# Two products of a gate/value round change places, and one subtraction moves ahead of a multiplication

## The chip, the core and the metric

The kernel runs on one core of a Trainium2 chip. The core has five engines, each with an instruction stream of its own: TensorE (PE; its weight loads are shown apart as PEld), VectorE (DVE), ScalarE (ACT), GpSimd (POOL) and SyncE (SP), whose queue issues most of the DMAs. They wait for one another through semaphores. What counts is the time of one execution on the device, in microseconds (us).

## What is computed

A DeltaNet recurrence (4 sequences, 8 heads, 768 tokens, head size 48) feeds a SwiGLU block (3072 tokens, 384 wide, 1536 inner). All values are fp32.

```python
def _attn_ref(q, k, v, beta):
    k_n = k / (np.linalg.norm(k, axis=-1, keepdims=True) + 1e-06)
    state = np.zeros((B, H, D, D), dtype=np.float32)
    for t in range(S):
        kt, vt, bt = (k_n[:, :, t], v[:, :, t], beta[:, :, t, None])
        y[:, :, t] = np.einsum('bhd,bhde->bhe', q[:, :, t], state)
        v_old = np.einsum('bhde,bhd->bhe', state, kt)
        state = state + bt[:, :, :, None] * np.einsum('bhd,bhe->bhde', kt, vt - v_old)
    return y

def _moe_ref(x, w_gate, w_val, w_out):   # x: y, heads side by side
    g = x @ w_gate
    silu = g * (1.0 / (1.0 + np.exp(-g)))
    return silu * (x @ w_val) @ w_out
```

## The kernel before

The 768 tokens are worked in 12 chunks of 64 (C), all four sequences at a time, so a chunk is 256 tokens. While the feed-forward part of chunk c runs, the attention of chunk c + 1 and the preparation of later chunks are woven into it: `point` and `point_and_fill` (lines 1757 to 1770) are places in the program at which one step of attention is issued, where one is due. The order of all instructions on all engines is written out by hand (`manual_schedule`, line 1807), so it is the order of the calls in the code.

The first two chunks use plain products with the gate and value weights while the weights are still being loaded and converted. From chunk 2 on (FAST) the gate and value products are made with a bilinear scheme that needs fewer products: for a round r, three blocks of 256 gate and value columns (`PAIRS[r]`), two halves of the chunk's tokens and three parts of the 384 rows are combined through sums of weights, sums of x and sums of partial results. There are two rounds in each of chunks 3 to 11 and one in chunk 2: 19 in all (`gate_val_fast`, line 1328).

A round consists of products numbered 0 to 14. `multiply(p, n, c, r)` (line 1291) issues product n: `product4` (line 1278) makes four fp32 matmuls of 128x128 weights by 128 tokens onto the four quarters of the PSUM bank p; in the trace each is two loads and two matmuls, so a product is eight of each, all on line 1280. Unless told to start afresh, a product adds onto what the bank holds. Products 1, 6, 7, 8, 9 and 12 (FORMS) read sums of weights that are reloaded from DRAM through a ring of four buffers; using one issues the DMA of a later one on SP's queue (line 1209). The other products, 0 and 5 among them, read blocks of `w_gv`, which stays in SBUF.

A round works in four PSUM banks: p4 (later called p2), p3 (later p6), p0 and p1 (later p5). `t0` and `t1` are 128x512 buffers in SBUF (`p_sb` in the trace; in the first round `last_h` and `h_f`). VectorE's `plus` and `minus` (lines 1506 to 1510) combine banks and buffers; their instructions are all on lines 1510 and 1507. `finish_h(c, r, e, p)` (line 1312) turns a finished bank into a piece of the hidden layer: ScalarE takes silu of the gate half (line 1316), VectorE multiplies it with the value half (line 1317).

The part of a round that matters here (lines 1357 to 1373), in words: products 7 (onto p1), 11 (onto p0) and 9 (onto p2); VectorE makes t1 = t1 - p0 behind product 11; product 0 completes bank p3 and product 5 adds onto p0; silu and multiplication finish p3; VectorE makes p5 = t0 - p0, which needs product 5, and p6 = t0 - p2, which overwrites bank p3. Then comes a point at which attention may be issued, and products 6 (onto p0), 10 (onto p5) and 8 (onto p6). These three wait for VectorE: 6 and 10 for the subtraction into p5, 8 for the one into p6. Product 5 overwrites what t1 = t1 - p0 reads, and waits for that. `load_late` (line 1349 and further on) issues a load of v on SP's queue when one is waiting there. Attention products read and write two pairs of banks of their own, `p_px` and `p_py`.

Behind the rounds, `output_fast` (line 1541) multiplies the hidden layer with the output weights in seven products (line 1557).

Of the kernel before, what the change touches and what calls it, by code (L numbers as in the profile page):

```python
# [20 lines left out]
def kernel(  # L21
# [327 lines left out]
    def load_late():  # L349
        if late_loads:  # L350
            late_loads.pop(0)()
# [811 lines left out]
    def new_h(c, f, at):  # L1163
        hs[c, f] = hp[at].rearrange("p (i n) -> p i n", i=2)
# [5 lines left out]
    def units(t):  # L1170
        return t.rearrange("p (u n) -> p u n", u=4)
# [17 lines left out]
    def block(k, r, n):  # L1189
        f = PAIRS[r][n]  # L1190
        return w_gv[:, :, k, 128 * f : 128 * f + 256]
# [8 lines left out]
    def form(n, c, r):  # L1200
        if c == FAST:
            return made_in[r][n]
        return slot(turns.index((c, r, n)))
# [7 lines left out]
    def used(n, c, r):  # L1211
        if c > FAST:
            reload(turns.index((c, r, n)) + len(ring))
# [35 lines left out]
    def x_of(c, tok_, k):  # L1249
        return xts[c][:, k, 128 * tok_ : 128 * tok_ + 128]  # L1250

    def x_less(c):
        return hp[4][:, 0:128] if c == FAST else x_of(c, 0, 0)
# [24 lines left out]
    def product4(p, w, moving, start=False):  # L1278
        for u in range(4):
            nc.tensor.matmul(  # L1280
                p[:, u], w(u), moving, start=start and u == 0, stop=True,
                skip_group_check=True,
            )
# [7 lines left out]
    def multiply(p, n, c, r, start=False):  # L1291

        if n in FORMS:
            t = units(form(n, c, r))
            w = lambda u: t[:, u]
        else:
            x = block(BLOCK[n][0], r, BLOCK[n][1])
            w = lambda u: x[:, u // 2, 128 * (u % 2) : 128 * (u % 2) + 128]
        if n == 11:
            moving = x_less(c)  # L1300
        else:
            moving = x_of(c, *PLAIN_X[n]) if n in PLAIN_X else sums_x[n]
        product4(p, w, moving, start)
        if n in FORMS:
            used(n, c, r)

    def temps(c, r):
        if (c, r) == (FAST, 0):
            return units(hp[13]), units(hp[5])
        return units(p_places[0][:, 0:HW]), units(p_places[0][:, HW : 2 * HW])  # L1310

    def finish_h(c, r, e, p):

        n = parts["sil"] = 1 - parts["sil"]
        silu_of = sil[:, n].rearrange("p (i n) -> p i n", i=2)
        nc.scalar.activation(silu_of, p[:, 0:2], ACTF.Silu)  # L1316
        nc.vector.tensor_tensor(  # L1317
            out=h_of(c, PAIRS[r][e % 3], e // 3), in0=silu_of, in1=p[:, 2:4], op=ALU.mult
        )
# [8 lines left out]
    def gate_val_fast(c, r, fill):  # L1328

        parts["x used"] = True  # L1330
        p4, p3, p0, p1 = (units(ffn_banks[i]) for i in parts["g"])
        p2, p6, p5 = p4, p3, p1
        t0, t1 = temps(c, r)
        assert (c, r) == (FAST, 0) or steps("join", 1) >= 4
        for f in PAIRS[r]:
            new_h(c, f, f // 2)

        tail = parts["tail"]
        if tail is not None:
            multiply(p4, 4, c, r, True)  # L1340
            nc.scalar.copy(p0, p4)
            tail[0]()
            multiply(p3, 13, c, r, True)
            nc.scalar.copy(t0, p3)
        multiply(p0, 1, c, r)
        if tail is not None:
            tail[1]()
        multiply(p4, 3, c, r)
        load_late()
        multiply(p3, 2, c, r)  # L1350
        nc.scalar.copy(t1, p4)
        plus(p1, p0, t0)
        plus(p2, p3, t1)
        if r > 0:
            sums_of_h(c, 6)
        point_and_fill(c + 1, 2.5, fill)
        multiply(p1, 7, c, r)
        multiply(p0, 11, c, r)
        nc.scalar.copy(t0, p1)
        multiply(p2, 9, c, r)  # L1360
        minus(t1, t1, p0)
        multiply(p3, 0, c, r)
        load_late()
        multiply(p0, 5, c, r)
        finish_h(c, r, 5, p3)
        minus(p5, t0, p0)
        minus(p6, t0, p2)
        point_and_fill(c + 1, 2.5, fill)
        multiply(p0, 6, c, r)
        multiply(p5, 10, c, r)  # L1370
        plus(t1, t1, p0)
        load_late()
        multiply(p6, 8, c, r)
        finish_h(c, r, 4, p5)
        finish_h(c, r, 1, p0)
        multiply(p2, 14, c, r)
        if r > 0:
            sums_of_h(c, 10)
        finish_h(c, r, 0, p6)
        finish_h(c, r, 3, p2)  # L1380
        if r > 0:
            sums_of_h(c, 8)
        point_and_fill(c + 1, 2.5, fill)

        def last():
            multiply(p6, 12, c, r)
            plus(t1, p6, t1)

        parts["tail"] = last, lambda: finish_h(c, r, 2, t1)
        a, b, m, d = parts["g"]  # L1390
        parts["g"] = (d, a, m, b)
# [114 lines left out]
    def minus(out, a, b):  # L1506
        nc.vector.tensor_tensor(out=out, in0=a, in1=b, op=ALU.subtract)  # L1507

    def plus(out, a, b):
        nc.vector.tensor_tensor(out=out, in0=a, in1=b, op=ALU.add)  # L1510
# [21 lines left out]
    def sums_of_h(c, f):  # L1532
        f1 = f - FH
        plus(s_of(f1), h_of(c, f1, 1), h_of(c, f, 1))
        minus(h_of(c, f1, 1), h_of(c, f1, 0), h_of(c, f1, 1))
# [147 lines left out]
    def steps(kind, *args):  # L1683
        return gens.get((kind, args), (None, 0))[1]
# [72 lines left out]
    def point_and_fill(c, n, fill):  # L1757
        spent.clear()
        point(c)
        fill(n - sum(spent))  # L1760
# [46 lines left out]
    with tc.manual_schedule(  # L1807
# [133 lines left out]
        for c in range(2, NCH):  # L1941
            if c > FAST:
                begin(c)
            point(c + 1)
            if c == FAST:
                begin(c)
            gate_val_fast(c, 0, fill)
            if c > FAST:
                gate_val_fast(c, 1, fill)
            else:  # L1950
                gate_val_plain(c, fill)
            output_fast(c, fill)
            finish(c + 1)
            x_sums(c + 1)
# [30 lines left out]
```

## Time and profile before

| what | value |
|---|---|
| median of 3 runs | 687.78 us (686.82 to 689.39) |
| the profiled execution | 689.76 us |
| its span, first to last instruction | 688.1 us |
| mean granted TensorE clock | 0.992 |
| matmuls of line 1280 by `x_t` with `w_gv` | 760, 102.4 us busy, 278 ns each |
| VectorE, middle and last subtraction of a round (`ffn<-p_sb,ffn`) | 36, 692 ns each |
| silu on ScalarE, line 1316 (`sil<-ffn`) | 95, 382 ns each |
| multiplication behind it, line 1317 (`h_f<-sil,ffn`) | 95, 418 ns each |

The profile is that of one execution. "Busy" is time in which an engine has work; matmuls are pipelined and overlap, so a busy TensorE is not one at its peak. The start of a weight load tells best when TensorE comes to a product. In the views, a line of a group or of the timeline gives engine, line of the code, operation, output and inputs by their names in the program, shape and count; what stands in square brackets is how long the engine was idle before, and what ended that.

### The profile page before, as it was taken

To read this page: it belongs to the slowest core of one execution; us is meant where nothing else is said; L and a number is where in the kernel's file an instruction comes from. 1 tells how busy PE (TensorE), PEld (TensorE's weight loads), DVE (VectorE), ACT (ScalarE), POOL (GpSimd) and SP (SyncE) were. 2 spreads that over 40 slices of the span, in tenths; PEclk is the share of its full clock that TensorE was granted. 3 is DMA by queue.
4 is the path that set the end of the run, shared out by engine and by line. 5 is a ranking of instruction groups with operands and counts; after the bars stand their busy time and mean duration, and the time that the engine had idled before them with its cause. 6 is when DMAs were issued, how large, how long until landed. Compare 5 with 4: busy or idle time off the path is not lost.

```text
span 688.1 us, 24813 instructions
## 1 busy us (share of the span) xinstructions
PE 653.7 (95%) x10850; PEld 603.7 (88%) x10850; DVE 473.3 (69%) x982; ACT 256.1 (37%) x546; POOL 201.7 (29%) x309
## 2 busy tenths in 40 slices
PE   7788999998999999999999999999999999999997
PEld 4566888756988899999999999999999999999997
DVE  7987778798569867757767747767657655645462
ACT  5785765214332332334332244332232333132130
POOL 7130031104883030881030881030882000000000
PEclk9998999999999999999999999999999999999999
DMA  9767824016226352276262176242187122132220
GB/s 135 169 176 190 243 94 137 1 35 136 45 45 164 73 136 64 49 156 143 54 134 74 45 153 138 60 110 80 26 171 152 48 88 78 40 100 71 76 71 23
DMA packets 147437, 68.55 MB, mean 100 GB/s; under 512 B 123457, under 2 KB 126561, under 8 KB 147329
## 3 DMA queue, kind: packets, MB, share of 16 engines
q1 hardware_dynamic: 144992, 66.48, 40.2%
q8 instruction: 85, 1.39, 0.8%
q10 hardware_dynamic: 2080, 0.39, 0.4%
q0 software_dynamic: 256, 0.10, 0.1%
q14 instruction: 24, 0.19, 0.1%
HBM read 59.08 MB, written 7.86 MB: 97 GB/s over the span
## 4 chain that ended last, share of the span: by engine, by line
PE 64%; DVE 3%; issue 0%; DVEq 0%
PE ffn L1280 36%; PE ffn L1557 17%; PE p_px L1073 1%; PE p_px L1054 1%; PE p_py L497 1%; PE p_py L1127 1%; PE p_py L1044 1%; DVE x_t L1510 1%; DVE ffn L1507 1%; PE p_px L902 1%; PE p_px L497 1%; PE p_py L1152 1%; PE p_py L884 1%; PE p_px L870 1%; DVE o_sb L1510 0%
## 5 line engine op out<-in xcount | busy, mean ns | idle before, releaser
L1280 PE MATMUL ffn<-x_t,w_gv 128*128 128x128 f32 x760 | 102.4, 278 | 6.6 <-DVE x_t L1507 6.6
L1280 PEld LDWEIGHTS ffn<-x_t,w_gv 128*128 128x128 f32 x760 | 93.1, 193 | 8.3 <-issue 5.8
L1557 PE MATMUL ffn<-wo_sb,h_f 128*128 128x192 f32 x480 | 84.2, 329 | 0.6 <-ACT ffn L1549 0.6
L811 POOL TENSOR_TENSOR n_b<-mb,half 128x32 f32<-128x32 f32 x5 | 27.6, 5520 | 191.3 <-DVE mb L551 191.3
L1280 PE MATMUL ffn<-x_ffn,w_gv 128*128 128x128 f32 x600 | 80.0, 277 | 0.0
L1557 PEld LDWEIGHTS ffn<-wo_sb,h_f 128*128 128x128 f32 x480 | 77.8, 190 | 1.6 <-ACT ffn L1549 0.9
L1316 ACT ACTIVATE sil<-ffn 128x256 f32<-128x256 f32 x95 | 34.5, 382 | 114.6 <-PE ffn L1280 106.6
L586 POOL TENSOR_TENSOR zb<-zb,h_f 128x31 f32<-128x31 f32 (+15 forms) x124 | 71.9, 580 | 9.7
L1280 PEld LDWEIGHTS ffn<-x_ffn,w_gv 128*128 128x128 f32 x600 | 73.8, 194 | 0.0
L580 POOL TENSOR_TENSOR h_f<-zb,mb 128x31 f32<-128x31 f32 (+15 forms) x124 | 69.4, 560 | 14.4 <-DVE mb L568 5.0
L1280 PE MATMUL ffn<-x_t,h_f 128*128 128x128 f32 x464 | 63.6, 280 | 3.9 <-DVE ffn L1507 3.9
L1317 DVE TENSOR_TENSOR h_f<-sil,ffn 128x256 f32<-128x256 f32 x95 | 37.6, 418 | 42.8 <-ACT sil L1316 42.8
L1280 PEld LDWEIGHTS ffn<-x_t,h_f 128*128 128x128 f32 x464 | 56.3, 192 | 5.9 <-DVE ffn L1507 4.9
L1440 PE MATMUL ffn<-x_ffn,w_gv 128*128 128x256 f32 x216 | 48.0, 381 | 0.0
L1440 PEld LDWEIGHTS ffn<-x_ffn,w_gv 128*128 128x128 f32 x216 | 40.7, 190 | 5.6
L1510 DVE TENSOR_TENSOR o_sb<-o_sb,ffn 128x192 f32<-128x192 f32 x49 | 17.1, 349 | 31.5 <-PE ffn L1557 31.0
L1510 DVE TENSOR_TENSOR ffn<-ffn,p_sb 128x512 f32<-128x512 f32 x36 | 24.8, 693 | 16.2 <-PE ffn L1280 15.1
L1557 PE MATMUL ffn<-last_k,h_f 128*128 128x192 f32 x200 | 35.8, 326 | 0.0
L1440 PE MATMUL ffn<-x_t,w_gv 128*128 128x256 f32 x144 | 35.7, 400 | 0.0
L1557 PEld LDWEIGHTS ffn<-last_k,h_f 128*128 128x128 f32 x200 | 32.8, 190 | 0.0
L1440 PEld LDWEIGHTS ffn<-x_t,w_gv 128*128 128x128 f32 x144 | 27.7, 199 | 4.0
L1280 PE MATMUL ffn<-x_ffn,h_f 128*128 128x128 f32 x224 | 30.0, 277 | 0.0
(343 smaller groups left out, 1165.2 us busy)
## 6 DMA issues: line engine op xcount, KB each, us to landing
h_f<-w_s SPq DMA_DIRECT2D x81, 256.0 KB, 2.7
more_w<-w_s SPq DMA_DIRECT2D x27, 256.0 KB, 2.9
vin<-in_v_dram SPq DMA_DIRECT2D x48, 96.0 KB, 3.5
out_dram<-o_sb SPq DMA_DIRECT2D x48, 96.0 KB, 2.2
kn<-in_k_dram SPq DMA_DIRECT2D x20, 192.0 KB, 4.7
w_s<-h_f SPq DMA_DIRECT2D x10, 256.0 KB, 3.2
zt<-in_moe_w_out_dram SPq DMA_DIRECT2D x6, 384.0 KB, 4.4
qpad<-in_q_dram SPq DMA_DIRECT2D x36, 64.0 KB, 3.2
```

The costliest lines, as they stand in the source:

```text
L497: nc.tensor.matmul(p_v[par][half_of(b if of_q else b ^ par), bp, j], kt[c][half_of(par), bp, j, b], xt[half_of(par), bp, j, b],)
L580: engine.tensor_tensor(out=t_v, in0=zb[:, 0 : j + 1, j : j + 1].to_broadcast([128, j + 1, m]), in1=mb[:, j : j + 1, j + 1 : R].to_broadcas ...
L586: engine.tensor_tensor(out=zb[:, 0 : j + 1, j + 1 : R], in0=zb[:, 0 : j + 1, j + 1 : R], in1=t_v, op=ALU.add,)
L811: nc.gpsimd.tensor_tensor(out=n, in0=mb.rearrange("p j i -> p (j i)")[:, 0 : R * R : R + 1], in1=half, op=ALU.pow,)
L870: nc.tensor.matmul(p_j[dst, c, m], a[lo, c, 2 * m + e, 0:R], zt[lo, c, 2 * m + e, R:C],)
L884: nc.tensor.matmul(p_j[hi, e, c, m], z1[row, c, m], t2[row, c, m])
L1280: nc.tensor.matmul(p[:, u], w(u), moving, start=start and u == 0, stop=True, skip_group_check=True,)
L1316: nc.scalar.activation(silu_of, p[:, 0:2], ACTF.Silu)
L1317: nc.vector.tensor_tensor(out=h_of(c, PAIRS[r][e % 3], e // 3), in0=silu_of, in1=p[:, 2:4], op=ALU.mult)
L1440: nc.tensor.matmul(ps[name][:, i], w_sb[:, t, (f + i) * 128 : (f + i + 1) * 128], xts[c][:, t], start=(t == 0 and i == 0), stop=(t == KT - 1),
L1510: nc.vector.tensor_tensor(out=out, in0=a, in1=b, op=ALU.add)
L1557: nc.tensor.matmul(p[x, part], a(f - f % 2)[:, f % 2], b(f), start=not begun and f == 0, stop=f == FH - 1, skip_group_check=True,)
```

## The change

In every round products 0 and 5 change places, and with them the order of the VectorE instructions behind them: p5 = t0 - p0 stands ahead of the multiplication of `finish_h(c, r, 5, p3)` instead of behind it. The late load stands between the two products as before.

```diff
         nc.scalar.copy(t0, p1)
         multiply(p2, 9, c, r)
         minus(t1, t1, p0)
+        multiply(p0, 5, c, r)
+        load_late()
         multiply(p3, 0, c, r)
-        load_late()
-        multiply(p0, 5, c, r)
+        minus(p5, t0, p0)
         finish_h(c, r, 5, p3)
-        minus(p5, t0, p0)
         minus(p6, t0, p2)
         point_and_fill(c + 1, 2.5, fill)
         multiply(p0, 6, c, r)
```

The instructions of ScalarE, GpSimd and SyncE keep their order; TensorE's and VectorE's change in the 19 rounds only, and their number stays.

## The prediction

> **What bounds the kernel now.** I read the page first: busy times, then the chain that ended last.
>
> ```profile
> PE 653.7 (95%) x10850; PEld 603.7 (88%) x10850; DVE 473.3 (69%) x982; ACT 256.1 (37%) x546; POOL 201.7 (29%) x309
> PE 64%; DVE 3%; issue 0%; DVEq 0%
> ```
>
> TensorE (PE) sets the time; VectorE (DVE) enters the chain only here and there. So the question is where TensorE stands still. The view of its waits, largest first:
>
> ```profile
> PE ffn L1280 <- DVE ffn L1507: 7.9, 10, 0.8
> PE ffn L1280 <- DVE x_t L1507: 6.6, 5, 1.8
> ```
>
> Ten times a product of line 1280 waits for a subtraction of line 1507. The timeline of one such round, in order of time (start, length, engine); I count from product 9's first weight load, 618.27:
>
> ```profile
> 618.27 0.97 PEld L1280 LDWEIGHTS ffn<-x_t,h_f 128*128 128x128 f32 x8
> 618.58 0.69 DVE L1507 TENSOR_TENSOR p_sb<-p_sb,ffn 128x512 f32<-128x512 f32 x1 [0.23 <-PE ffn L1280]
> 619.17 0.97 PEld L1280 LDWEIGHTS ffn<-x_ffn,w_gv 128*128 128x128 f32 x8
> 620.06 0.97 PEld L1280 LDWEIGHTS ffn<-x_t,w_gv 128*128 128x128 f32 x8
> 620.37 0.38 ACT L1316 ACTIVATE sil<-ffn 128x256 f32<-128x256 f32 x1 [2.10 <-PE ffn L1280]
> 620.78 0.42 DVE L1317 TENSOR_TENSOR h_f<-sil,ffn 128x256 f32<-128x256 f32 x1 [1.51 <-ACT sil L1316]
> 621.26 1.29 DVE L1507 TENSOR_TENSOR ffn<-p_sb,ffn 128x512 f32<-128x512 f32 x2
> 622.01 0.97 PEld L1280 LDWEIGHTS ffn<-x_t,more_w 128*128 128x128 f32 x8 [0.98 <-DVE ffn L1507]
> 622.01 1.16 PE L1280 MATMUL ffn<-x_t,more_w 128*128 128x128 f32 x8 [0.79 <-DVE ffn L1507]
> 622.90 0.97 PEld L1280 LDWEIGHTS ffn<-x_t,w_gv 128*128 128x128 f32 x8
> ```
>
> The loads are products 9, 0, 5, 6, 10. A product holds TensorE 0.89 (619.17 to 620.06). Product 6 would load at 620.95 and loads at 622.01: a pause of **1.06**. Why: VectorE starts on a product's result 1.20 after that product's first load (620.06 to 621.26; 622.01 to 623.21 for the next one agrees), the middle subtraction (p5 = t0 - p0) takes 0.69, and TensorE's load follows 0.06 after its end (621.95 to 622.01). Product 5 is directly in front of product 6, so 1.20 + 0.69 + 0.06 = 1.95 must pass where 0.89 is covered. The multiplication ends at 621.20, just as product 5's result is ready, so today it costs nothing.
>
> There are 19 rounds (18 + 1 first subtractions in the answer on line 1507):
>
> ```profile
> L1507 DVE TENSOR_TENSOR p_sb<-p_sb,ffn x18: 686/687/690, 239.6 to 661.8; 128x512 f32<-128x512 f32 x18
> L1507 DVE TENSOR_TENSOR h_f<-h_f,ffn x1: 689/689/689, 182.5 to 182.5; 128x512 f32<-128x512 f32 x1
> ```
>
> I went through all in the timeline. **Ten are open** (product 9 at 182.2, 239.3, 312.2, 343.3, 416.3, 447.3, 519.3, 618.3, 647.1, 661.5): nothing stands between products 5 and 6, and each shows the picture above. **Nine are filled**: TensorE has 1.1 to 2.2 us of attention products there and shows no pause. In six of these, and in all open ones, the first subtraction (t1 = t1 - p0) runs from 0.31 to 1.00. In three (256.5, 360.6, 464.6) it is late:
>
> ```profile
> 255.90 1.22 DVE L888 COPY zt<-p_py 32x1024 f32<-32x1024 f32 x1 [0.70 <-ACT zt L888]
> 256.54 0.97 PEld L1280 LDWEIGHTS ffn<-x_t,h_f 128*128 128x128 f32 x8
> 257.16 0.69 DVE L1507 TENSOR_TENSOR p_sb<-p_sb,ffn 128x512 f32<-128x512 f32 x1
> ```
>
> A copy of 1.22 stands in front, and the subtraction ends at 257.85, 1.31 after product 9's load.
>
> **The change, step by step.** No instruction is added or removed, and no DMA: products 5 and 0 take weights that stay in w_gv, so they issue no reload, and the late load keeps its place in SP's queue between the reloads of products 9 and 6. ScalarE's order is the same. What moves is the wait of product 5 (it adds onto p0, so it waits for the first subtraction): it loses its cover, product 0. Behind it in TensorE's queue is everything.
>
> *Open round.* The first subtraction ends at 1.00, so product 5 loads at 1.06 instead of 0.89: new pause 0.17. Product 0 loads at 1.95. The middle subtraction starts at 1.06 + 1.20 = 2.26, with no multiplication ahead of it, and ends at 2.95; product 6 loads at 3.01. By TensorE's own pace it would be 1.95 + 0.89 = 2.84, so a second pause of 0.17. Before, product 6 loaded at 622.01 - 618.27 = 3.74. Gain **0.73**, ten times: 7.3.
>
> Next late would be product 8, which overwrites p3 and waits for the last subtraction. Silu starts at 1.95 + 1.20 = 3.15, the multiplication 0.41 later (620.37 to 620.78), ends at 3.98; the subtraction starts 0.03 after it (617.92 behind a 0.42 operation at 617.47, where one VectorE operation waits for another), ends at 4.70, product 8 could load at 4.76. TensorE comes to it at 3.01 + 2 x 0.89 = 4.79. Cover 0.03: I cost it at nothing. Bounds: 0 if VectorE starts earlier, as the second of the pair above does (1.29 for two of 0.69), and 0.1 a round, 1.0 in all, if something comes between.
>
> *Filled round.* Only the new pause of product 5 counts; the attention products cover the rest. Six times 0.17 is 1.0. In the three late rounds product 5 loads at 1.31 + 0.06 = 1.37 instead of 0.89: three times 0.48 is 1.4. Bounds for the lateness of the copy: nothing, or again as much (1.4).
>
> *What VectorE has behind.* The last subtraction ends 0.42 later against product 9 (4.70 for 4.28) and TensorE is 0.73 earlier, so VectorE's later work comes 1.15 closer. The tightest place I found is the open round at 312.2: two transposes of 1.2 stand behind the subtraction, and the multiplication of the p5 bank ends only at 319.71; the next user of that bank on TensorE starts at 321.78. Of 2.07 cover 0.92 is left. ScalarE's silu of product 0 comes about 1.06 later; in the filled round at 567.85 it then ends at 571.4, before the next copy there (571.95). Both cost nothing; each tenth missing in the ten open rounds would cost 1.0.
>
> [...] Here the wait sits on the load: the waiting load and its first matmul start together at 622.01, so I keep 0.17.
>
> Sum: -7.3 + 1.0 + 1.4 = **-4.9 us**. The profiled execution took 689.76 with a span of 688.1; that is 2.0 above the median of the three runs shown, 687.78, and I take the same pauses to be in those runs. From the span it makes 683.2; from the median: **682.9**, 0.7% faster.
>
> **The rivals.**
>
> *The weights go ahead* (0.05). Product 5's matmuls, not its loads, wait: pause 1.06 - 1.01 = 0.05, and the same arithmetic gives 0.06 before product 6. Gain 0.95 x 10, cost 6 x 0.05 + 3 x 0.36 = 1.4: -8.1, time 679.7. For it: loads overlap matmuls everywhere. Against: 622.01 twice, above. [...]
>
> *VectorE is late at the first subtraction* (0.05). The place is product 5, now without cover. If every round were as late as the three (0.31), the pause is 0.48 everywhere: open rounds gain 0.41 x 10, filled ones lose 0.48 x 9, together +0.2, time 688.0. From 0.3 on the change turns slower; at twice that (0.62) the pause is 0.79: -1.0 + 7.1 = +6.1, time **693.9**. For it: three rounds do it already. Against: in the other sixteen VectorE stands idle before that subtraction (0.23, as above, up to 3.15), and what precedes it is not touched.
>
> *The gain is given back* (0.07). Four more waits for the x sums (1.2 each, chunk starts at 230, 285, 389 and 493) would swallow what was won since the last one, if they were set by something that does not move: of the rounds before 493, 6 x 0.73 - 3 x 0.48 - 2 x 0.17 = 2.6 is lost, time 685.5. Against: those sums start behind an addition that TensorE's own product releases, so they move along.
>
> *Many short pauses throttle the clock* (0.01). The trace has a stretch at half clock shortly ahead of the first round:
>
> ```profile
> 172.20:175.40 3.20, 3.20 (x15) 3.20 (x16) 3.10 (x8) 0.57 (x1) 2.81 (x6) 0.50 0.01 2
> 618.20:626.00 7.80, 7.01 (x62) 6.82 (x61) 4.69 (x11) 1.61 (x6) 0.00 (x0) 1.00 0.36 104
> ```
>
> (The seventh figure is the granted clock.) One such stretch a round would cost half of 3.2, nineteen times: +30, time 718. Against: pauses of 1.06 leave the clock at 1.00. [...]
>
> That the order does not change is no rival: both engines run a fixed order, and all 19 rounds have the new one.
>
> **How the numbers follow.** Forecast 0.80, rivals 0.05, 0.05, 0.07, 0.01, and 0.02 for what I did not see. The forecast's own bounds: 1.0 for product 8, 1.4 either way for the late copy, about 1 for how the median of a few runs falls (686.82 to 689.39 shown). The range 680.5 to 685.7 holds it and the given-back case. This kernel's measurement can tell about 0.5%, 3.4 us, from no change. Faster: 0.75 of the forecast's 0.80 and the weights' 0.05 minus a little, 0.79; slower 0.05; same 0.16.
>
> **What would show it.** In an open round of the changed kernel: loads of 9, 5, 0, 6 at 0, 1.06, 1.95, 3.01, and 10 and 8 at 0.89 steps behind; waits of line 1280 for line 1507 in nearly all 19 rounds but about 0.2 each, with some 5 us less in sum and pause; no pause before product 8. It is wrong if product 5's pause is several tenths in most rounds, if product 8 or the first product behind a round waits, or if the x-sum waits grow.

## The result, and the profile after

| | median of 20 runs | lowest to highest |
|---|---|---|
| before | 689.17 us | 686.05 to 694.58 |
| changed | 685.33 us | 682.12 to 691.74 |

The ratio of the two is 0.9946, with a 95% interval of 0.992 to 0.9971: the change is worth 3.7 us (2.0 to 5.5 by the interval). The two medians lie 3.84 apart. The forecast was 4.9. The time itself, 685.33, is 2.4 above the 682.9 that was forecast: 1.4 of it is the kernel before, whose median was 687.78 in the three runs that the forecast started from and is 689.17 in these twenty; the rest is the smaller gain. The profiled execution of the changed kernel took 688.78 us with a span of 687.1, 3.4 above the median. Its page, the line of the engines and the chain that ended last, shows the same picture as before:

```profile
PE 657.7 (96%) x10850; PEld 605.8 (88%) x10850; DVE 474.4 (69%) x982; ACT 256.5 (37%) x546; POOL 196.7 (29%) x309
...
PE 62%; DVE 4%; issue 1%; ACT 0%; DVEq 0%
```

TensorE still sets the end. What is new in the chain is 1% of "issue", in which TensorE waited for nothing that the profile shows; that is taken up below. In the view of TensorE's waits (us in total, times, longest), the line of ten waits and 7.9 us for the subtractions of line 1507 into a bank is gone. What is left of that line of code is the x sums, as before, and three short waits for `p_sb`:

```profile
PE ffn L1280 <- DVE x_t L1507: 6.8, 5, 1.8
...
PE ffn L1280 <- DVE p_sb L1507: 0.6, 3, 0.2
```

The same view of the weight loads, from 183.8 to 662 us, has the short pauses that stand in its place, nine of 0.15 before product 6 and three of 0.4 before product 5 in the late rounds (the tenth of the first kind, at 664.3, lies behind this stretch; the 0.16 before product 5 elsewhere is not listed there, the loads' starts show it):

```profile
PEld ffn L1280 <- DVE ffn L1507: 1.4, 9, 0.2
PEld ffn L1280 <- DVE p_sb L1507: 1.2, 3, 0.4
```

This is the round that the prediction showed, in the timeline of the changed kernel (start, length, engine; lines of other engines are left out):

```profile
619.32 0.97 PEld L1280 LDWEIGHTS ffn<-x_t,h_f 128*128 128x128 f32 x8
...
619.63 0.69 DVE L1507 TENSOR_TENSOR p_sb<-p_sb,ffn 128x512 f32<-128x512 f32 x1 [0.24 <-PE ffn L1280]
620.37 0.97 PEld L1280 LDWEIGHTS ffn<-x_t,w_gv 128*128 128x128 f32 x8
...
621.26 0.97 PEld L1280 LDWEIGHTS ffn<-x_ffn,w_gv 128*128 128x128 f32 x8
...
621.64 0.70 DVE L1507 TENSOR_TENSOR ffn<-p_sb,ffn 128x512 f32<-128x512 f32 x1 [1.32 <-PE ffn L1280]
622.39 0.97 PEld L1280 LDWEIGHTS ffn<-x_t,more_w 128*128 128x128 f32 x8 [0.15 <-DVE ffn L1507]
...
622.88 0.42 DVE L1317 TENSOR_TENSOR h_f<-sil,ffn 128x256 f32<-128x256 f32 x1 [0.54 <-ACT sil L1316]
623.28 0.97 PEld L1280 LDWEIGHTS ffn<-x_t,w_gv 128*128 128x128 f32 x8
623.34 0.70 DVE L1507 TENSOR_TENSOR ffn<-p_sb,ffn 128x512 f32<-128x512 f32 x1
...
624.17 0.97 PEld L1280 LDWEIGHTS ffn<-x_t,h_f 128*128 128x128 f32 x8
```

Counted from product 9's load (619.32), products 5, 0, 6, 10 and 8 load at 1.05, 1.94, 3.07, 3.96 and 4.85; the forecast was 1.06, 1.95, 3.01 and two steps of 0.89. All ten open rounds read so. Product 6 comes 3.74 - 3.07 = 0.67 earlier than before instead of 0.73, because the middle subtraction starts at 2.32 and not at 2.26. Product 8 does not pause: the last subtraction ends at 4.72 (623.34 + 0.70), and TensorE comes at 4.85.

In six filled rounds product 5 loads at 1.05, 0.16 later than the product that stood there. The three late rounds behave as forecast, with the copy of 1.22 in front:

```profile
256.80 1.22 DVE L888 COPY zt<-p_py 32x1024 f32<-32x1024 f32 x1 [0.70 <-ACT zt L888]
...
257.43 0.97 PEld L1280 LDWEIGHTS ffn<-x_t,h_f 128*128 128x128 f32 x8
...
258.05 0.69 DVE L1507 TENSOR_TENSOR p_sb<-p_sb,ffn 128x512 f32<-128x512 f32 x1
258.80 0.86 PEld L1280 LDWEIGHTS ffn<-x_t,w_gv 128*128 128x128 f32 x7 [0.39 <-DVE p_sb L1507]
```

Product 5 loads 258.80 - 257.43 = 1.37 behind product 9, where 0.89 was TensorE's own pace.

To leave the start of the program aside (the first load of line 1280 is at 172.18 in the trace of before and at 173.86 in that of after, through the same instructions), I call **length** the time from that load to TensorE's last load. It is 510.99 before and 508.34 after: 2.65 shorter. The two traces, laid side by side load by load, give the terms:

| term | forecast, us | measured, us |
|---|---|---|
| ten open rounds | -7.3 | -6.7 |
| filled rounds: six, and three late ones | +1.0 +1.4 | +2.34 |
| chunk 3's start: the x sums wait 0.31 longer (1.2 to 1.5), product 7 another 0.32; a stop of 0.34 for "issue" that the trace of before has at 234.2 is gone | 0 | +0.3 |
| the output's third product (line 1557) waits in two chunks | 0 | +0.3 |
| TensorE stops inside a block of attention products at 352 | not foreseen | +0.93 |
| TensorE stops at 250.3 | not foreseen | +0.22 |
| sum | -4.9 | -2.6 |

Without the two stops the measured terms add up to -3.8, which is what the medians of 20 runs show. That may be chance: the interval, 2.0 to 5.5, holds the sum with the stops as well, so the times can't tell how large a part the stops have in the typical run.

### The profile page after: what moved, and what is told of

It reads as the page before. It is cut to its first block, busy times and chain, and to the rows that moved or that the text cites. A ratio compares the mean times of both kernels' runs of the same rounds, so it can differ in the third digit from the quotient of the medians.

```text
span 687.1 us, 24832 instructions
## 1 busy us (share of the span) xinstructions
PE 657.7 (96%) x10850; PEld 605.8 (88%) x10850; DVE 474.4 (69%) x982; ACT 256.5 (37%) x546; POOL 196.7 (29%) x309
## 3 DMA queue, kind: packets, MB, share of 16 engines
q8 instruction: 85, 1.39, 0.9%
## 4 chain that ended last, share of the span: by engine, by line
PE 62%; DVE 4%; issue 1%; ACT 0%; DVEq 0%
PE ffn L1280 35%; PE ffn L1557 17%; PE p_px L1073 1%; PE p_px L1054 1%; PE p_py L1127 1%; PE p_py L1044 1%; PE p_py L497 1%; DVE x_t L1510 1%; PE p_px L902 1%; PE p_py L1152 1%; PE p_px L870 1%; PE p_py L884 1%; PE p_px L497 1%; DVE zt L888 1%; ACT zt L888 0%
## 5 line engine op out<-in xcount | busy, mean ns | idle before, releaser
L580 POOL TENSOR_TENSOR h_f<-zb,mb 128x31 f32<-128x31 f32 (+15 forms) x124 | 71.0, 573 | 14.4 <-DVE mb L568 5.0
L586 POOL TENSOR_TENSOR zb<-zb,h_f 128x31 f32<-128x31 f32 (+15 forms) x124 | 69.9, 564 | 9.7
L1507 DVE TENSOR_TENSOR ffn<-p_sb,ffn 128x512 f32<-128x512 f32 x36 | 25.1, 696 | 24.4 <-PE ffn L1280 23.8
```

The source lines that it names most:

```text
L580: engine.tensor_tensor(out=t_v, in0=zb[:, 0 : j + 1, j : j + 1].to_broadcast([128, j + 1, m]), in1=mb[:, j : j + 1, j + 1 : R].to_broadcas ...
L586: engine.tensor_tensor(out=zb[:, 0 : j + 1, j + 1 : R], in0=zb[:, 0 : j + 1, j + 1 : R], in1=t_v, op=ALU.add,)
```

## The experiments

The theory was the prediction's: the gain is the multiplication's and product 0's places taken together, since what counts is the time from product 5's load to product 6's. The first four kernels take the change apart. The length of each is compared with 510.99 of before. Each ratio is to runs of the kernel before that were made together with the experiment (medians 687.69, 688.90 and 689.85 us).

**The products alone, VectorE's order as before.**

```diff
+        multiply(p0, 5, c, r)
+        load_late()
         multiply(p3, 0, c, r)
-        load_late()
-        multiply(p0, 5, c, r)
         finish_h(c, r, 5, p3)
         minus(p5, t0, p0)
         minus(p6, t0, p2)
```

> Products 0 and 5 change places in all rounds, VectorE keeps its old order. My theory: the middle subtraction now stands behind a multiplication that waits for product 0, which is the later product. Counted from product 9's first load, product 5 loads at 1.05 and 0 at 1.94, the multiplication ends at 3.98, the middle subtraction runs from 4.01 to 4.71 and product 6 loads at 4.76, against 3.74 before: ten open rounds lose 1.02 each, the three filled rounds with only one attention product group lose 0.8, 0.8 and 0.7, the other filled ones 3 x 0.16 and 3 x 0.47. Together +14 us, ratio 1.021. Rival: the order of the products is what brings the gain and VectorE's order is an accompaniment; then ratio about 0.995, as for the whole change.

Measured: 702.49 us, ratio 1.0195 (1.0146 to 1.0244). An open round in the timeline of this kernel, product 5's load at 627.03:

```profile
627.03 0.97 PEld L1280 LDWEIGHTS ffn<-x_t,w_gv 128*128 128x128 f32 x8
627.91 0.97 PEld L1280 LDWEIGHTS ffn<-x_ffn,w_gv 128*128 128x128 f32 x8
629.12 0.38 ACT L1316 ACTIVATE sil<-ffn 128x256 f32<-128x256 f32 x1 [3.14 <-PE ffn L1280]
629.53 0.42 DVE L1317 TENSOR_TENSOR h_f<-sil,ffn 128x256 f32<-128x256 f32 x1 [2.56 <-ACT sil L1316]
629.87 1.29 DVE L1507 TENSOR_TENSOR ffn<-p_sb,ffn 128x512 f32<-128x512 f32 x2
630.61 0.52 PEld L1280 LDWEIGHTS ffn<-x_t,more_w 128*128 128x128 f32 x4 [1.73 <-DVE ffn L1507]
```

VectorE stands idle for 2.56, in the last 1.3 of it with product 5's result ready (627.03 + 1.20 = 628.23): its next instruction is the multiplication, which waits for silu of the product that now comes second. The weight loads stand idle for 1.73 ahead of product 6 instead of 0.98. Product 6 loads at 4.64 after product 9, not at the 4.76 that was expected, since the subtractions start 0.34 behind the multiplication's start, before its 0.42 are over. The length grows by 13.3: 10 x 0.90 in the open rounds, 2.3 in the filled ones for product 5, and 1.4 because in three filled rounds (product 9 at 549.4, 567.9 and 602.3 in the trace of before) the attention products no longer cover the longer wait; a stop of 0.69 for "issue" at 523.6 comes on top, less some small pieces. The rival that the swap of products alone brings the gain has fallen.

**VectorE's order alone, the products as before.**

```diff
         multiply(p3, 0, c, r)
         load_late()
         multiply(p0, 5, c, r)
+        minus(p5, t0, p0)
         finish_h(c, r, 5, p3)
-        minus(p5, t0, p0)
         minus(p6, t0, p2)
```

> Only VectorE's order changes: the middle subtraction stands ahead of the multiplication, the products keep their old order. My theory: before, the subtraction started when product 5 was ready, not when the multiplication was done, so nothing is won. It now waits for TensorE and for ScalarE's copy in two steps and starts 0.07 later, at 3.06 after product 9's load; product 6 loads at 3.81 instead of 3.74. Ten times +0.07, +0.7 us, ratio 1.001, no change that can be measured. Rival: the multiplication held the subtraction back; then product 6 would load up to 0.5 earlier in the open rounds, -5 us, ratio 0.993.

Measured: 690.55 us, ratio 1.0036 (1.0007 to 1.0065). TensorE's waits in this kernel:

```profile
PE ffn L1280 <- DVE ffn L1507: 8.6, 10, 0.9
```

Ten waits as before, 0.07 longer each (8.6 for 7.9). Product 6 loads at 3.81, 0.07 later than before. So the multiplication was not in the subtraction's way, as the prediction had it (it ended at 621.20, the result was ready at 621.26); moving the subtraction in front of it alone costs a little. The ratio is above the expected 1.001, which its interval still holds. Of the 1.90 that the length grows by, the ten waits make 0.7; the rest are stops of TensorE for "issue" (0.57 at 352, 0.44 at 519.9, 0.18 at 509.2). The 0.07 is taken up below. Neither half is worth anything; together they are.

**Open rounds only, and filled rounds only.** The order is chosen by the round; OPEN lists the ten, and the second kernel has `not in`:

```diff
+        if (c, r) in OPEN:
             multiply(p0, 5, c, r)
...
+        else:
             multiply(p3, 0, c, r)
```

> The whole change in the ten open rounds alone; the nine filled ones keep the old order. My theory: each open round gains 0.67 (product 6 loads at 3.07 for 3.74) and the filled rounds' cost of 6 x 0.16 + 3 x 0.47 = 2.3 us is gone: -6.7 us, ratio 0.990, and loads in the filled rounds at 0.89 and 1.79 as before. Rival: the pauses of the filled rounds cost nothing, because what follows them has time to spare; then the ratio is that of the whole change, 0.995.

> The complement: the change in the nine filled rounds alone. My theory: +2.3 us, ratio 1.0034, product 5 loading at 1.05 in six of them and at 1.36 in the three late ones, and all ten open rounds as before with product 6 at 3.74. Rival: filled rounds cost nothing, ratio 1.000.

Measured: open only 684.53 us, ratio 0.9941 (0.9912 to 0.9969); filled only 691.74 us, ratio 1.0041 (1.0011 to 1.0071). The filled rounds alone make the length 2.66 longer, 2.33 of it before product 5 in the nine rounds, which settles their price: the rival that attention products hide it has fallen. Open only misses its expected ratio of 0.990, though its rounds read as expected (product 6 at 3.07; 0.89 and 1.79 in the filled ones): its length is 506.11, 4.9 shorter than before instead of 6.7. Between these lie a stop of 1.16 at the same attention block as in the changed kernel, twice 0.14 at the output's third product, and 0.4 in smaller pieces. By time it can't be told from the whole change; by the trace it is 2.2 shorter (508.34 to 506.11).

**Why the middle subtraction starts 0.07 late.** In both the changed kernel and the one before, this subtraction is to read `t0`, ScalarE's copy. Before, the multiplication in front of it had already waited for ScalarE. Now the subtraction is the first on VectorE that does so, and it waits for TensorE too. The view of line 1507 by source counts semaphore instructions of VectorE's sequencer, before:

```profile
L1507 DVEq EVENT_SEMAPHORE  x22: 21/21/21, 153.8 to 670.9; - x22
```

and after:

```profile
L1507 DVEq EVENT_SEMAPHORE  x41: 21/21/21, 155.3 to 670.0; - x41
```

There are 19 more, one a round. The theory: one of the two waits now stands in an instruction of its own ahead of the subtraction, so the subtraction follows TensorE's release 0.07 later. In the records of the round shown above, the added instruction waits for TensorE's semaphore and runs from 621.58 to 621.60, and the subtraction, which itself waits for ScalarE's, starts at 621.64. The experiment lets a tiny VectorE operation read one column of `t0` while VectorE is idle, behind the first subtraction; that is added work.

```diff
         minus(t1, t1, p0)
+        nc.vector.tensor_copy(seen, t0[:, 0, 0:1])
         multiply(p0, 5, c, r)
```

> The whole change, and behind the first subtraction a VectorE copy of one column of t0, which does nothing but wait for ScalarE's copy into t0 while VectorE has nothing else to do. My theory: in the changed kernel the middle subtraction starts 1.27 after product 5's load and not 1.20, because it waits for two engines and the second wait is an instruction of its own behind product 5; with the early look only TensorE's wait is left, so it starts at 2.25 instead of 2.32 after product 9's load and product 6 loads at 3.00 instead of 3.07 in the open rounds, 0.7 us in all. Rival: the 0.07 comes from something else (ScalarE or TensorE using PSUM at that moment); then 2.32 and 3.07 stay.

Measured, in the timeline of an open round of this kernel (product 9's load at 620.00):

```profile
620.00 0.97 PEld L1280 LDWEIGHTS ffn<-x_t,h_f 128*128 128x128 f32 x8
...
620.92 0.15 DVE L1364 COPY seen<-p_sb 128x1 f32<-128x1 f32 x1
...
622.25 0.69 DVE L1510 TENSOR_TENSOR ffn<-p_sb,ffn 128x512 f32<-128x512 f32 x1 [1.19 <-PE ffn L1280]
623.00 0.97 PEld L1280 LDWEIGHTS ffn<-x_t,more_w 128*128 128x128 f32 x8
```

The subtraction starts at 2.25 and product 6 loads at 3.00, in all ten open rounds: the forecast's 2.26 and 3.01. The added semaphore instructions are gone too; the line of the subtractions, 1510 in this kernel, has as many as before the change:

```profile
L1510 DVEq EVENT_SEMAPHORE  x22: 21/21/21, 155.8 to 670.4; - x22
```

The theory stands. The length is 508.33, no shorter than the changed kernel's, since this run stops 1.15 in the attention block and in other places; its one run, of 689.28 us, says nothing on the time.

**Giving product 5 cover.** What is left in a round is 0.16 before product 5 and 0.24 before product 6 (3.07 less 1.94 and 0.89). Two kernels put other products into these gaps. The first moves product 11, whose result the first subtraction needs, ahead of product 7 in every round; the second orders the open rounds 11, 7, 5, 0, 9, with the sums of the hidden layer (`sums_of_h`) behind the first subtraction and the late load behind product 9, and leaves the filled rounds as they were before the change.

```diff
+        multiply(p0, 11, c, r)
         multiply(p1, 7, c, r)
-        multiply(p0, 11, c, r)
         nc.scalar.copy(t0, p1)
```

> The whole change, and product 11 ahead of product 7, so that two products and not one stand between product 11 and product 5. My theory: product 5's new pause goes in the sixteen rounds in which VectorE is on time and stays at 0.47 in the three late ones. Counted from the group's first load (product 11): 5 at 2.67, 0 at 3.57, 6 at 4.69 against 5.52 before, a gain of 0.83 in the ten open rounds; filled rounds lose only 3 x 0.47 = 1.4. Together -6.9 us, ratio 0.990. Rival: the pause of 0.16 is not the wait for the first subtraction but a price of the other order of products as such; then -4.4, ratio 0.994 as for the whole change.

```diff
+        if (c, r) in OPEN:
+            multiply(p0, 11, c, r)
+            multiply(p1, 7, c, r)
+            nc.scalar.copy(t0, p1)
+            minus(t1, t1, p0)
+            multiply(p0, 5, c, r)
+            multiply(p3, 0, c, r)
+            if r > 0:
+                sums_of_h(c, 6)
+            multiply(p2, 9, c, r)
+            load_late()
+            minus(p5, t0, p0)
+            finish_h(c, r, 5, p3)
+            minus(p6, t0, p2)
+        else:
...
```

> In the ten open rounds the order 11, 7, 5, 0, 9, and the sums of h that stood ahead of the first subtraction behind it; the filled rounds as before the change. My theory: two products now stand between product 5 and product 6, more than the 1.20 + 0.07 + 0.70 + 0.05 that the middle subtraction needs, so the pause ahead of product 6 goes altogether and only 0.16 ahead of product 5 is left. From the group's first load: 5 at 1.94, 0 at 2.84, 9 at 3.73, 6 at 4.62 against 5.52 before. Gain 0.90 x 10 = 9.0 us, ratio 0.987. Rival: the time set free is taken by what VectorE has behind (last subtraction, sums, transposes), so that product 8 or the next round's products wait; then the ratio stays near 0.990.

Measured: 11 first 686.28 us, ratio 0.9957 (0.9929 to 0.9984); 9 last **681.67 us, ratio 0.9892 (0.9866 to 0.9918)**, the fastest of all; its interval lies below that of the changed kernel (0.992 to 0.9971). An open round of the latter, with products 7, 5, 0, 9 and 6:

```profile
611.69 0.97 PEld L1280 LDWEIGHTS ffn<-x_t,h_f 128*128 128x128 f32 x8
...
612.75 0.97 PEld L1280 LDWEIGHTS ffn<-x_t,w_gv 128*128 128x128 f32 x8
...
613.63 0.97 PEld L1280 LDWEIGHTS ffn<-x_ffn,w_gv 128*128 128x128 f32 x8
614.01 0.70 DVE L1525 TENSOR_TENSOR ffn<-p_sb,ffn 128x512 f32<-128x512 f32 x1 [0.53 <-PE ffn L1280]
614.53 0.97 PEld L1280 LDWEIGHTS ffn<-x_t,h_f 128*128 128x128 f32 x8
...
615.42 0.75 PEld L1280 LDWEIGHTS ffn<-x_t,more_w 128*128 128x128 f32 x6
```

Two products now lie between 5 and 6, the subtraction ends at 614.71, and product 6 loads at TensorE's own pace, 0.89 behind product 9. The only pause left is 0.17 before product 5. The length is 504.04, 6.95 shorter than before, where the ten rounds are worth 9.1 by their loads. Stops of 0.81, 0.29, 0.25 and 0.20 take 1.55 (the longest, at 399.1, the profile puts down to a VectorE operation that had ended 0.55 earlier), and 0.5 goes to waits for VectorE at chunk 3's start and in the output part ahead of it. So the rival is right for about 0.5; product 8 does not wait, it loads 0.89 behind product 10.

The kernel with 11 first has its rounds as expected too (no pause before product 5 in 16 of 19), but only 4.3 of the 6.9 that they are worth shows in its length, 506.66: stops of 0.68, 0.75 and 0.27 at three places, 0.5 at chunk 3's start and ahead of it and twice 0.15 at the output take the rest. Its ratio would fit the rival's 0.994 and not the 0.990 of the theory; the loads rule the rival out, since the pause of 0.16 is gone with products 5 and 0 in the new order.

**The stop at 352.** TensorE's part of the timeline there, in the changed kernel:

```profile
351.08 1.12 PE L870 MATMUL p_px<-zt,a_sb 32*32 32x32 f32 x108
352.91 0.38 PE L870 MATMUL p_px<-zt,a_sb 32*32 32x32 f32 x20 [0.71 <-issue]
```

and before:

```profile
350.78 1.29 PE L870 MATMUL p_px<-zt,a_sb 32*32 32x32 f32 x128
```

A block of 128 small products breaks off behind the 108th, and what released it is "issue", so no semaphore that the profile shows. By the weight loads' starts the stop is 0.93. I suspected SP's queue: the late load of q between this round's products 5 and 0 might delay something. The experiment moves that load behind product 14 in this round, once in the changed kernel and once in the fastest one.

```diff
-        load_late()
+        if (c, r) != (5, 0):
+            load_late()
         multiply(p3, 0, c, r)
...
         multiply(p2, 14, c, r)
+        if (c, r) == (5, 0):
+            load_late()
```

> The whole change, and in the first round of chunk 5 alone the eight small loads of blocks of q are issued behind product 14 instead of between products 5 and 0. In the changed kernel's profile the attention products of line 870 that follow this round stand still for 0.93 in the middle of their block, released by nothing that the profile shows, about 1.3 behind the end of a 16 KB transfer of the queue of kind instruction; in the profile before they run through. My theory: TensorE waits for its own instructions there, and their transfer stands behind the loads of q; with the loads later the block of line 870 runs through in 1.2 and 0.9 us are won, ratio about 0.993 to 0.995 (too little for the time to show). Rival: the stop has to do with the place in the program alone; then it stays at the same instruction whatever the loads do.

> The kernel with the order 11, 7, 5, 0, 9 in the open rounds, with the same eight loads later. My theory: as that kernel or up to 0.3 us faster (its stop in line 870 was 0.26), ratio 0.987 to 0.990 against before. Rival: the later loads delay the transposes of q that need them in the next chunk, and TensorE with them; then slower than that kernel by a few tenths of a per cent.

Measured: the whole change with the load moved 689.34 us, ratio 0.9984 (0.9958 to 1.001); the fastest kernel with it 682.61 us, ratio 0.989 (0.986 to 0.992). The stop stays (0.97 and 0.56), in each behind the same instruction as in the kernel that it was made from, and the second kernel shows no delay from the later loads in its time. In the first of the two another 0.86 went at 512.0 and 0.49 at 251.7. So moving the load does not help. It does not clear the loads of q, though. A 16 KB packet of the instruction queue ends 1.3 to 1.5 ahead of the end of this stop in all nine traces that have it; in the changed kernel it runs from 350.67 to 351.61 with the loads of q issued from 346.76 to 352.57, and with the load moved from 352.20 to 353.17 with them issued from 350.36 to 355.71. They surround the packet both times. Whether they delay its start is not settled.

What points to the place in the program is the profile page's line on the DMA queue of kind instruction (packets, MB, share):

```profile
q8 instruction: 85, 1.39, 0.8%
```

That is 16 KB a packet (1.39 MB in 85). Count TensorE's weight loads, matmuls and its sequencer's instructions (waits for semaphores, and three drains) in order: 21857 in the traces of before and after. From 180 us on, the eleven traces have 30 places at which both load and matmul are released by "issue" and the load follows the one ahead of it by over 0.1 more than in the quickest of the traces. All 30 stand 193 or 194 behind a multiple of 256 in that count, and a stream of 21857 has 85 such places, as many as there are packets. The stop at 352 comes two or three loads later in the three kernels with product 11 first, which have five or six of the sequencer's instructions fewer ahead of it; its place in the count is the same. Each of the 30 ends 1.2 to 1.8 us behind the end of a packet. I take these to be the places where the next packet's instructions begin; no view shows which instructions a packet holds. The block at 352 runs its 256 instructions in 1.2 us where it does not stop, and meets one such place.

The size of the stop there differs from trace to trace: none before and with the products alone; 0.57 with VectorE's order alone; 0.93 after; 1.16 (open only), 0.19 (filled only), 1.15, 0.68, 0.26, 0.97 and 0.56 in the rest. That the long pauses of before gave the packet time to arrive is a tendency in these at most: before and the products alone have long pauses and no stop, but VectorE's order alone has pauses longer than before's and a stop, and the filled rounds alone keep the long pauses and have a short one. In the trace of before and in that of the products alone the packet ends at 349.90 and 351.29, 1.8 and 1.3 ahead of the load at that place (351.69 and 352.63), so it is there in time. By these traces the size of the stop follows from how late the packet comes; what makes it late stays open.

## Why the prediction was right, and where its sizes were off

- **What bounds the kernel, and the mechanism**: right. From product 5's load to product 6's 2.02 pass in the round shown (620.37 to 622.39): 1.27 to the subtraction's start, its 0.70, and 0.05 to the load; product 0 in between covers 0.89 of it. The two kernels with one half each show that it takes both edits: the products alone cost 2%, VectorE's order alone gains nothing (0.4% slower, of which its ten waits explain 0.1%).
- **Open round, 0.73**: mis-sized. It is 0.67, ten times 6.7 for 7.3. The failing step is "Product 0 loads at 1.95. The middle subtraction starts at 1.06 + 1.20 = 2.26". The 1.20 came from subtractions that had only TensorE to wait for. In its new place the subtraction is the first to need ScalarE's copy as well, and that wait, in an instruction of its own, makes it 1.27. With the wait taken away it was 2.25.
- **Product 5's lost cover**: right. 0.16 in six filled rounds and 0.47 in three, 2.34 in all for 2.4; the kernel with the filled rounds alone has 2.33 there, 2.66 in length and ratio 1.0041.
- **Product 8, cover 0.03, costed at nothing**: right, and nearly as narrow as it was said to be. The last subtraction ends at 4.72, product 8 could load at 4.78, and TensorE comes at 4.85: a cover of 0.07, most of it from product 6's delay of 0.06. With that delay taken away, in the kernel with the added copy, product 8 still did not wait in nine of the ten rounds, and waited 0.05 in the first.
- **"Both cost nothing"**, on what VectorE and ScalarE have behind: off by 0.3. The prediction followed the p5 bank through VectorE to its next user on TensorE, and there it was right: in the changed kernel the multiplication ends at 321.65 and the user starts at 322.62, 0.97 for the forecast's 0.92. It did not follow ScalarE, whose copies and silus shift with VectorE, to the clear of an output bank (line 1549) that stands behind them in its queue. In the changed kernel:

```profile
324.60 0.74 ACT L525 COPY a_sb<-p_px 32x256 f32<-32x256 f32 x2
...
325.24 0.31 ACT L1549 COPY ffn<-mask_q 128x192 f32<-128x192 f32 x1
...
325.60 1.11 PEld L1557 LDWEIGHTS ffn<-last_h,h_f 128*128 128x128 f32 x7
```

The clear ends at 325.55 and the output's third product loads at 325.60, 0.15 late. It happens twice, behind the open rounds at 312.2 and 416.3, which have two transposes behind them, and not in all ten.
- **The gain is given back** (a rival at 0.07): true in one place of the four and for a small part. The x sums at 230 wait 1.5 instead of 1.2, since VectorE has no idle time from 221 to 237 and does not move along, and product 7 of the same round loses 0.32 more; a stop of 0.34 that is gone there makes up for half of it. The waits for x sums in all grew by 0.2 (6.8 for 6.6).
- **VectorE late at the first subtraction** and **the weights go ahead** (0.05 each): neither. The subtraction runs from 0.31 in the open rounds as before; product 5's loads themselves wait, at 1.05 and not at 0.89, and its first load and first matmul start 0.01 apart in the round shown (620.37 and 620.38).
- **Many short pauses throttle the clock** (0.01): no. The mean granted clock was 0.982 to 0.995 in the profiles of all these kernels, with 0.990 for the one with the longest pauses; in the trace of the changed kernel it is 1.00 from 178 to 686 us, and so at every place where the two products were exchanged.
- **Not foreseen at all**: the stops for "issue", 1.15 in the profiled execution. They are the main reason why its length shrank by 2.65 only; the medians of 20 runs are nearer to the terms without them, which the interval is too wide to make more of.
- **The time, 682.9**: within the range by 0.4 only. The prediction took the median of before from three runs; twenty put it 1.4 higher, and that alone uses up half of the room to the upper bound (685.7).

## What to carry to other kernels

When a consumer waits on another engine, count what lies between the producing and the waiting instruction on the bounding engine, and move independent work in there; then see that the helper engine's order follows, since half the edit may cost more than the whole gains (here 2.0% for 0.5%). Where the move makes an instruction the first to need a second engine's result, add something for the extra wait (here 0.07), or let an operation in an idle moment take it. Put the move only where nothing else covers the wait: here nine rounds that were covered paid a third of what the other ten won.

## What the runs showed of the hardware

In this kernel a VectorE wait for a second engine cost 0.07: as an instruction of its own ahead of the subtraction (0.02 in the records) it put the subtraction's start 0.07 later in all ten open rounds, and a copy of 0.15 in idle time that took one of the two waits brought that back. TensorE's 30 stops for "issue" all stand 193 or 194 behind a multiple of 256 in the count of its instructions, and end 1.2 to 1.8 us behind the end of a packet of 16 KB on the queue of kind instruction. Where 256 instructions run in 1.2 us it stopped for 0.2 to 1.2 us in nine of eleven traces. What makes a packet late stays open.
